# A top-32 search on VectorE: the order of two rows' instructions in a step is changed, with two candidate buffers, and two small operations are rewritten

## The chip, the cores and the metric

The kernel runs on one core of one Trainium2 chip. A core has five engines that run side by side: TensorE (PE, with its weight loads as PEld), VectorE (DVE), ScalarE (ACT), GpSimd (POOL) and SyncE (SP), which here issues most of the DMAs. Each engine works through its own list of instructions in order and waits on semaphores where it needs another's result, or an earlier one of its own. The metric is the device time of one execution in microseconds (us); smaller is better.

## The reference

An attention whose softmax keeps only the 32 largest scores of each row is followed by a mixture of eight experts with one expert per token. Cut to what matters:

```python
scores = (q @ k.transpose(0, 1, 3, 2)) / np.sqrt(64)        # 8 batches, 8 heads, 576 x 576
kth = np.partition(scores, -32, axis=-1)[..., -32:-31]
scores = np.where(scores >= kth, scores, -1e9)
attn = softmax(scores); x = attn @ v                        # rows of 512, 4608 tokens
logits = x @ w_gate; e = argmax(logits)                     # one of 8 experts
out = softmax(logits)[e] * (np.maximum(x @ w1[e], 0) @ w2[e])
```

The part that concerns us is finding, for each of the 8 x 8 x 576 score rows, the 32 largest of 576 values.

## The kernel before

**Tiling and stages.** The score rows are worked in 144 steps (`NQ * NT` = 16 x 9). A step t holds two tiles of 128 rows by 576 scores, called row 0 and row 1 here. The loop at L1004 issues, in each pass t, work of several steps at once: the scores of step t+3 on PE (L1012 to L1017), copied into an `sb` pair by ACT; the top-32 search of step t on DVE; the mask of step t-2 (a Sign on ACT at L454 and an add of 576 columns on POOL at L455); the transposes of step t-3 on PE (L461), the exponentials (L467) and the product with v (L477) after that. The experts follow the attention; there the work is mostly matmuls (L1153, L1168).

**The search of one step** (`topk`, L407). Row 0 is cut into 11 chunks and row 1 into 10 (`CHUNKS`). A MAX8 on each chunk (list `one`, run at L1025) writes its 8 largest values into a candidate tile, `cand0` (88 columns) or `cand1` (80 columns). The candidates are laid out so that column groups hold the chunks' first, second, ... largest values. Then each row has four rounds on its candidates (list `two`, run at L1033): a MAX8 gives 8 of the 32 values into `vq`, and a match_replace takes these 8 out of the candidates before the next round. On the chip a match_replace is two instructions, MATCH_VALUE_LOAD, which reads the 8 values just found, and MATCH_REPLACE8. The rounds read 22, 33, 77 and 88 columns of row 0 and 20, 40, 70 and 80 of row 1 (`RANKS`). So a row has seven entries in `two`, written in this text as a0 to a6 for row 0 (a0, a2, a4, a6 are MAX8, a1, a3, a5 match_replace) and b0 to b6 for row 1. Each entry needs the one before it of its own row. The order before is a0 b0 a1 b1 ... a6 b6, behind all 21 chunks. The chunks are called c0 to c20 (c0 to c10 of row 0).

**Small instructions.** Other jobs put small DVE instructions into a queue (`vec`, `dq`). From the third entry of `two` on, one of them is issued behind each entry (L1034), and what is left behind the last entry. In some steps the queue is empty, in others it holds up to 27.

**Behind the search.** `last`, a small POOL operation that makes two biases `nb` out of `vq`, is kept as `delayed` and issued at the start of the next pass (L1007). In the last step of a group of nine a TENSOR_REDUCE `mx_n` (L430) is added behind b6.

**Two small operations** matter as well. `settle` (L440) computes a shift for several groups: one scalar_tensor_tensor of 3 columns for each group, with `slope` and `level` as its two tensors. `j_find` (L656) computes a list of places `r_fl`, one column, as li[:,1] * 37 + li[:,0], with a scalar_tensor_tensor whose two tensors are two columns of `r_li`. It runs once in each of the eight batches.

Of the kernel before, what the change touches and what calls it, by code (L numbers as in the profile page):

```python
# [8 lines left out]
F32 = mybir.dt.float32  # L9
# [5 lines left out]
OP = mybir.AluOpType  # L15
# [5 lines left out]
NEG = -3.0e38  # L21
BELOW = 1.0 - 2.0 ** -24
TOPK = 32
# [25 lines left out]
def attention_moe(ctx, tc, q, k, v, w_gate, w1, w2, out):  # L49
    nc = tc.nc  # L50
# [37 lines left out]
    NT = 2 * MAIN + 1  # L88
# [6 lines left out]
    work = att.enter_context(tc.tile_pool(name="work", bufs=2))  # L95
# [53 lines left out]
    NLT = HP * (2 * MAIN + 1)  # L149
# [18 lines left out]
    for i in range(3):  # L168
        t = consts.tile([128, S], BF, name=f"sg{i}")
# [20 lines left out]
    shift = consts.tile([128, NQ, 3], F32, name="shift")  # L190
    slope = consts.tile([128, 3], F32, name="slope")
    nc.vector.memset(slope, 1.0)
    nc.vector.memset(slope[:, 0:1], -0.125)
    level = consts.tile([128, 3], F32, name="level")
# [18 lines left out]
    for p in range(HP):  # L213
        for h in range(2):
            hd = 2 * p + h
            w = 2 * MAIN + 1
            t0 = 1 + (p // 2) * 2 * w + (h if p % 2 == 0 else w + 1 + h)
            a = attr[:, t0:t0 + 2 * MAIN - 1:2, :]
# [4 lines left out]
            a = attr[h * LEFT:(h + 1) * LEFT, tl_, :]  # L223
# [8 lines left out]
    for i in range(3):  # L232
        t = work.tile([128, 2, KW], F32, name=f"qk{i}", bufs=1)
# [11 lines left out]
    for i in range(2):  # L245
        t = jobs.tile([128, NLT + 1, 2], F32, name=f"nb{i}", bufs=1)
# [32 lines left out]
    def flush(queue):  # L279
        while queue:  # L280
            queue.pop(0)()
# [60 lines left out]
    def grp(t):  # L342
        if t < 0 or t >= steps:
            return []
        n, s = divmod(t, NT)
        p = 2 * n
        if s < MAIN:
            return [p * NT + s, p * NT + MAIN + s]
        if s == MAIN:
            return [p * NT + 2 * MAIN, (p + 1) * NT + 2 * MAIN]  # L350
        s -= MAIN + 1
        return [(p + 1) * NT + s, (p + 1) * NT + MAIN + s]
# [54 lines left out]
    def topk(t, us):  # L407
        n, s = divmod(t, NT)
        if s == 0:
            VQ[n] = jobs.tile([128, 2 * NT, TOPK], F32, name="vq")  # L410
        v = VQ[n][:, 2 * s:2 * s + 2, :]
        one, two, cand = [], [], {}
        for i, u in enumerate(us):
            nc_ = CHUNKS[i]
            cand[i] = work.tile([128, 8 * nc_], F32, name=f"cand{i}", bufs=1)
            for c in range(nc_):
                one.append((nc.vector.max, (cand[i][:, c::nc_], SB[u][:, edges[i][c]:edges[i][c + 1]])))

        for r in range(TOPK // 8):
            w = [cand[i][:, 0:CHUNKS[i] * RANKS[i][r]] for i in range(2)]  # L420
            for i in range(2):
                two.append((nc.vector.max, (v[:, i, 8 * r:8 * r + 8], w[i])))
            if r < TOPK // 8 - 1:
                for i in range(2):
                    two.append((nc.vector.match_replace, (w[i], v[:, i, 8 * r:8 * r + 8], w[i], NEG)))
        b, lt = divmod(t, 2 * NT)
        nb = NB[t] = NBB[b % 2][:, 1 + 2 * lt:3 + 2 * lt]
        if s == NT - 1 and n + 4 < NQ:
            MX[n] = jobs.tile([128, 1], F32, name="mx_n")
            two.append((nc.vector.tensor_reduce, (MX[n], VQ[n][:, :, 0], AX.X, OP.max)))  # L430

        last = (nc.gpsimd.tensor_tensor, (nb, v[:, :, 0:TOPK:TOPK - 1], factors, OP.mult))
        return one, two, last
# [6 lines left out]
    def settle(pt, ns, done):  # L440
        mm = jobs.tile([128, 1], F32, name="mm")
        vec(nc.vector.tensor_reduce, mm, pt[:, 0:128], axis=AX.X, op=OP.max)
        vec(done)
        for n in ns:
            vec(nc.vector.scalar_tensor_tensor, shift[:, n], slope, mm, level, op0=OP.mult, op1=OP.add)

    SHIFTED = {0, 1, 2, 3}

# [165 lines left out]
    def j_find(b):  # L614
        sm = lambda name, shape, dt=F32: jobs.tile(shape, dt, name=name, bufs=1)
        yield need(dve=0.3)
        while (b + 1) * NLT // (2 * NT) - 1 not in CHECKED:
            yield
        key = sm("r_key", [128, NLT])
        vec(nc.vector.scalar_tensor_tensor, key, CNT[b], float(2 * TOPK - S), idx1, op0=OP.not_equal, op1=OP.mult)  # L620
        vec(nc.vector.max, rhs[:, :, 0], key)
        ok = sm("r_ok", [128, 9], BF)
        vec(nc.vector.tensor_scalar, ok[:, 0:8], rhs[:, :, 0], 0.0, None, op0=OP.is_gt, op1=OP.add,
            accum_out=ok[:, 8:9])
        nbb = NBB[b % 2]
        ntab = dram.tile([128 * (NLT + 1), 2], F32, name=f"ntab{b}")
        nc.sync.dma_start(ntab.rearrange("(p t) a -> p t a", p=128), nbb)
        yield need(spot=1, pe=0.1)
        pr, leave = spot("stat")
        pe(nc.tensor.matmul, pr[:, 0:1], before, ok[:, 8:9], start=True, stop=True)  # L630
        pe(nc.tensor.matmul, pr[:, 1:3], ones, ok[:, 7:9], start=True, stop=True)
        act(nc.scalar.activation, stat[:, b], pr[:, 0:3], AF.Copy)
        if 2 * b + 4 < NQ:
            spread(pr[:, 128:256])
            settle(pr[:, 128:256], [2 * b + 4, 2 * b + 5], leave)
            SHIFTED.update([2 * b + 4, 2 * b + 5])
        else:
            act(leave)
        yield need(slack=1)
        yield need(dve=1.3)  # L640
        sl = sm("r_sl", [128, 8], BF)
        vec(nc.vector.scalar_tensor_tensor, sl, slots[:, 0:8], stat[:, b, 0:1], ok[:, 0:8], op0=OP.add, op1=OP.mult)
        oh = sm("r_qx", [128, 512]).bitcast(BF).rearrange("p (j x) -> p j x", j=8)
        vec(nc.vector.tensor_tensor, oh, slots[:, None, :].to_broadcast([128, 8, 128]),
            sl[:, :, None].to_broadcast([128, 8, 128]), op=OP.is_equal)
        yield need(spot=1, pe=0.5)
        pl, leave = spot("li")
        for j in range(8):
            pe(nc.tensor.matmul, pl[:, 0:2], oh[:, j], rhs[:, j], start=(j == 0), stop=(j == 7))
        li = sm("r_li", [128, 2])  # L650
        act(nc.scalar.activation, li, pl[:, 0:2], AF.Copy)
        act(leave)
        yield need(slack=1)
        yield need(dve=0.1)
        fl = sm("r_fl", [128, 1], I32)
        vec(nc.vector.scalar_tensor_tensor, fl, li[:, 1:2], float(NLT + 1), li[:, 0:1], op0=OP.mult, op1=OP.add)  # L656
        yield need(pool=2.0)
        at = sm("r_at", [128, 4], I32)
        pool(nc.gpsimd.indirect_dma_start, out=at, out_offset=None, in_=atab,
             in_offset=bass.IndirectOffsetOnAxis(ap=fl[:, 0:1], axis=0))  # L660
        nb = jobs.tile([128, 8], F32, name="r_nb", bufs=3)
        pool(nc.gpsimd.indirect_dma_start, out=nb[:, 0:2], out_offset=None, in_=ntab,
             in_offset=bass.IndirectOffsetOnAxis(ap=fl[:, 0:1], axis=0))
        yield need(pool=1.8)
        qi = jobs.tile([128, 2], I32, name="r_qi", bufs=3)
        pool(nc.gpsimd.tensor_scalar, qi, at[:, 0:3:2], b * H * S, None, op0=OP.add)
        sb = jobs.tile([128, S], F32, name="r_sb", bufs=2)
        pool(nc.gpsimd.indirect_dma_start, out=sb, out_offset=None, in_=SCD[b],
             in_offset=bass.IndirectOffsetOnAxis(ap=at[:, 0:1], axis=0))
        hf = sm("r_hf", [128, 1])  # L670
        pool(nc.gpsimd.tensor_copy, hf, at[:, 1:2])
        hm = jobs.tile([128, H], F32, name="r_hm", bufs=3)
        pool(nc.gpsimd.tensor_scalar, hm, eight, hf, None, op0=OP.is_equal)
        hmb = hm[:, :, None].to_broadcast([128, H, D])
        pool(nc.gpsimd.tensor_scalar, used[:, b:b + 1], hf, float(H), None, op0=OP.is_lt)
        yield need(pool=0.7)

        low = nb[:, 2:3]
        pool(nc.gpsimd.tensor_scalar, nb[:, 3:4], nb[:, 1:2], 1.0 + 2.0 ** -10, None, op0=OP.mult)
        pool(nc.gpsimd.tensor_scalar, low, nb[:, 0:1], -(2.0 ** -7), None, op0=OP.mult)  # L680
        pool(nc.gpsimd.tensor_tensor, low, low, nb[:, 3:4], op=OP.add)
        FOUND[b] = (sb, nb, qi, hmb)
# [314 lines left out]
    if NQ > 1:  # L997
# [2 lines left out]
    prep(2)  # L1000
    AHEAD = [(A0, ahead_load, (0,)), (A0, ahead_load, (1,)), (A1, ahead_take, ()), (A2, ahead_split, (0,)),
             (A3, ahead_split, (1,))]
    delayed = None
    for t in range(steps + LAG + TD + 4):  # L1004
        n, s = divmod(t, NT)
        if delayed:
            delayed[0](*delayed[1])  # L1007
        if grp(t - LAG - TD - 1):
# [10 lines left out]
            transp(t - LAG - TD)  # L1019
        flush(pq)  # L1020
        flush(aq)
        one, two, last = topk(t, grp(t)) if grp(t) else ([], [], None)
        for m in range(max(len(one), 1)):
            if m < len(one):
                one[m][0](*one[m][1])  # L1025
        delayed = last
        if t == 1:
            settle(first_pt, [0, 1, 2, 3], lambda: release(first_pt))
            mine_, dq[:] = dq[:], []
            flush(mine_)  # L1030
        mine, dq[:] = dq[:], []
        for m, (f, a) in enumerate(two):
            f(*a)  # L1033
            if mine and m >= 2:  # L1034
                mine.pop(0)()
# [458 lines left out]
```

## Time and profile before

| what | value |
|---|---|
| median of the runs | 1287.82 us (three runs, 1287.07 to 1288.76) |
| the profiled execution's own time | 1287.93 us |
| its span, first to last instruction | 1286.1 us |
| DVE busy | 1032.4 us in the span |
| first and last chunk MAX8 of the search | 12.8 us and 752.2 us |
| MAX8 on chunks | 3024 (144 x 21) |

The attention takes the time up to some 755 us; the experts take the rest. The profile is of one execution; its time lies 0.11 us above the median of the runs. In a row of the timeline the first number is the start in us from the span's start, the second how long the merged group lasted; then come the engine, the line of the kernel, the operation, the tiles and shapes and how many instructions were merged (x2). Two DVE instructions overlap in such rows: the next one starts before the one ahead has ended, so the cost of one on its engine is the distance from its start to the next start, and not its length.

### The profile page before, as it was taken

To read this page: it belongs to the slowest core of one execution; us is meant where nothing else is said; L and a number is where in the kernel's file an instruction comes from. 1 tells how busy PE (TensorE), PEld (TensorE's weight loads), DVE (VectorE), ACT (ScalarE), POOL (GpSimd) and SP (SyncE) were. 2 spreads that over 40 slices of the span, in tenths; PEclk is the share of its full clock that TensorE was granted. 3 is DMA by queue.
4 is the path that set the end of the run, shared out by engine and by line. 5 is a ranking of instruction groups with operands and counts; after the bars stand their busy time and mean duration, and the time that the engine had idled before them with its cause. 6 is when DMAs were issued, how large, how long until landed. Compare 5 with 4: busy or idle time off the path is not lost.

```text
span 1286.1 us, 31773 instructions
## 1 busy us (share of the span) xinstructions
PE 1211.3 (94%) x9126; PEld 962.8 (75%) x9126; DVE 1032.4 (80%) x6907; ACT 831.2 (65%) x1699; POOL 840.5 (65%) x1213
## 2 busy tenths in 40 slices
PE   6999999999999999999999879899999999999997
PEld 3667667766666676666766668788999898899996
DVE  7999999999999999999999987756674333446555
ACT  4999798888888888888988853333333232334433
POOL 4676766767867867867967858765655142445654
PEclk8999999999999999999999999899999999999999
DMA  6765565655655655655654635646565243556773
GB/s 169 234 177 184 172 192 154 187 172 160 179 172 160 184 169 169 180 173 155 204 172 140 185 98 156 205 130 182 163 185 177 70 131 90 164 162 186 231 211 114
DMA packets 276759, 215.38 MB, mean 167 GB/s; under 512 B 136617, under 2 KB 218713, under 8 KB 276576
## 3 DMA queue, kind: packets, MB, share of 16 engines
q1 hardware_dynamic: 265840, 190.11, 50.1%
q0 software_dynamic: 9504, 22.86, 5.7%
q8 instruction: 74, 1.21, 0.4%
q14 instruction: 109, 0.89, 0.2%
q10 hardware_dynamic: 1232, 0.30, 0.1%
HBM read 106.69 MB, written 107.90 MB: 167 GB/s over the span
## 4 chain that ended last, share of the span: by engine, by line
DVE 51%; PE 37%; issue 3%; POOL 3%; DMA 2%; ACT 2%; SPq 1%; POOLq 0%; ACTq 0%; DVEq 0%
DVE cand L1025 25%; PE ph L1153 17%; PE y L1168 17%; DVE cand L1033 11%; DVE vq L1033 9%; PE mt L1133 1%; PE pt L265 1%; DVE xm L265 1%; POOL sb L455 1%; POOL wl L957 1%; ACT sg L454 1%; DVE r_v L265 1%; DMA rk<-in_k_dram 1%; DVE r_qx L265 1%; SPq L113 0%
## 5 line engine op out<-in xcount | busy, mean ns | idle before, releaser
L455 POOL TENSOR_TENSOR sb<-sb,sg 128x576 f32<-128x576 f32 x288 | 370.4, 1303 | 43.2 <-ACT sg L454 39.7
L1025 DVE MAX8 cand<-sb 128x8 f32<-128x52 f32 (+2 forms) x3024 | 368.3, 207 | 0.2 <-issue 0.2
L957 POOL TENSOR_TENSOR wl<-r,wh 128x512 fp32r<-128x512 f32 x118 | 152.7, 1295 | 206.3 <-DVE wh L956 202.0
L454 ACT ACTIVATE sg<-sb,nb 128x576 int8<-128x576 f32 x288 | 229.2, 796 | 61.0 <-POOL sb L455 60.5
L1154 ACT ACTIVATE hh<-ph 128x256 fp32r<-128x256 f32 (+3 forms) x136 | 58.2, 428 | 247.4 <-PE ph L1153 209.7
L477 PEld LDWEIGHTS px<-et,rv 128*64 128x64 f32 x2688 | 129.2, 137 | 118.4 <-ACT xt L265 50.4
L1033 DVE MAX8 vq<-cand 128x8 f32<-128x22 f32 (+7 forms) x1152 | 200.2, 204 | 0.0
L461 PE MATMUL tt<-turner,sb 128*128 128x128 f32 x1296 | 176.0, 277 | 22.6 <-POOL sb L455 17.9
L367 PE MATMUL ps<-qk 64*128 64x512 f32 (+1 forms) x576 | 183.7, 646 | 4.3 <-ACT sb L369 3.5
L1155 DVE SCALAR_TENSOR_TENSOR hl<-ph,hh 128x256 fp32r<-128x256 f32 (+3 forms) x136 | 65.0, 478 | 151.3 <-ACT hh L1154 131.9
L467 ACT ACTIVATE et<-tt,shift 128x1152 f32<-128x1152 f32 x144 | 178.3, 1238 | 1.5 <-PE tt L461 1.5
L477 PE MATMUL px<-et,rv 128*64 128x128 f32 (+1 forms) x2688 | 162.2, 266 | 11.2 <-ACT xt L265 8.7
L461 PEld LDWEIGHTS tt<-turner,sb 128*128 128x128 f32 x1296 | 145.6, 143 | 35.7 <-POOL sb L455 29.0
L1153 PE MATMUL ph<-xh,wh 128*128 128x256 f32 (+3 forms) x536 | 169.8, 317 | 0.0
L1153 PE MATMUL ph<-xh,wl 128*128 128x256 f32 (+3 forms) x536 | 165.8, 309 | 0.0
L1153 PE MATMUL ph<-xl,wh 128*128 128x256 f32 (+3 forms) x536 | 165.3, 308 | 0.0
L1033 DVE MATCH_REPLACE8 cand<-vq,cand 128x22 f32<-128x22 f32 (+2 forms) x864 | 158.5, 189 | 0.0
L369 ACT ACTIVATE sb<-ps 128x1024 f32<-128x1024 f32 x144 | 149.1, 1035 | 8.1 <-PE ps L367 8.1
L1168 PE MATMUL y<-wh,hl 128*128 128x512 f32 x324 | 128.4, 396 | 1.4 <-DVE skip L265 1.4
L1168 PE MATMUL y<-wl,hh 128*128 128x512 f32 x324 | 128.2, 396 | 0.0
L1168 PE MATMUL y<-wh,hh 128*128 128x512 f32 x324 | 128.2, 396 | 0.0
L1153 PEld LDWEIGHTS ph<-xh,wh 128*128 128x128 f32 x536 | 101.6, 190 | 4.2 <-issue 1.3
(260 smaller groups left out, 2183.4 us busy)
## 6 DMA issues: line engine op xcount, KB each, us to landing
r<-in_moe_w_dram SPq DMA_DIRECT2D x236, 256.0 KB
sc<-sb SPq DMA_DIRECT2D x128, 288.0 KB
sc<-sb SPq DMA_DIRECT2D x128, 256.0 KB
rv<-in_v_dram SPq DMA_DIRECT2D x32, 256.0 KB
xs<-xm SPq DMA_DIRECT2D x16, 512.0 KB
rq<-in_q_dram SPq DMA_DIRECT2D x60, 128.0 KB
rk<-in_k_dram SPq DMA_DIRECT2D x60, 128.0 KB
sc<-sb SPq DMA_DIRECT2D x32, 144.0 KB
```

Source lines behind the costliest of these rows:

```text
L367: nc.tensor.matmul(MAINS[:, n], qk[:, 0, w], qk[:, 1, 2 * LEFT:], start=True, stop=True)
L369: nc.scalar.activation(bass.AP(EX[-1].tensor, EX[-1].offset, [list(EX[-1].ap[0]), [S + LEFT, 2], [1, M]]), MAINS, AF.Copy)
L454: nc.scalar.activation(upper(SG[i]), SB[u], AF.Sign, bias=nb[:, i, 1:2], accum_out=CNT[b][:, 2 * lt + i:2 * lt + i + 1])
L455: nc.gpsimd.tensor_tensor(SB[u], SB[u], SG[i], op=OP.add)
L461: nc.tensor.matmul(tt[:, c], x[:, c * 128:(c + 1) * 128], ident, start=True, stop=True, is_transpose=True)
L467: nc.scalar.activation(ET[t], three.rearrange("p (c q) -> p c q", c=NB9), AF.Exp, bias=shift[:, t // NT, 0:1], scale=0.125)
L477: yield lambda kb=kb, blk=blk: nc.tensor.matmul(px[h * 64:(h + 1) * 64], block(rv, p % 2, kb if kb < MAIN else MAIN + n, h), et[:, blk, q] ...
L957: ((other or nc.gpsimd) if i else nc.vector).tensor_tensor(lo, r, hi, op=OP.subtract)
L1025: one[m][0](*one[m][1])
L1033: f(*a)
L1153: nc.tensor.matmul(ph, a[:, c, :], x[:, c, s], start=(m == 0), stop=(m == len(seq) - 1))
L1168: nc.tensor.matmul(PY[u, t], a[:, s], x, start=(f == 0 and m == 0), stop=(f == FC - 1 and m == 2))
```

## The change

Four things are done.

1. The order. c0 of a step is issued first in the pass, ahead of `delayed` and the rest. Behind it comes b6 of the step before (`carry`). Then c1 to c18 follow, and `two` is now a0 c19 a1 c20 a2 b0 a3 b1 a4 b2 b3 a5 b4 a6 b5. In the last step of a group of nine, b6 is not carried but follows b5 directly, and `mx_n` follows where there is one.
2. `cand0` and `cand1` have two buffers each, used in turn by the steps.
3. `settle` writes the shifts of all its groups with one instruction, with `slope` and `level` broadcast over the groups.
4. `r_fl` is computed by a tensor_scalar, with one column of `r_li` as its tensor and the other as its scalar operand for each partition.

The diff in full, but for context lines:

```diff
-        one, two, cand = [], [], {}
+        one, two, cand, rounds = [], [], {}, ([], [])
...
-            cand[i] = work.tile([128, 8 * nc_], F32, name=f"cand{i}", bufs=1)
+            cand[i] = work.tile([128, 8 * nc_], F32, name=f"cand{i}", bufs=2)
...
             for i in range(2):
-                two.append((nc.vector.max, (v[:, i, 8 * r:8 * r + 8], w[i])))
-            if r < TOPK // 8 - 1:
-                for i in range(2):
-                    two.append((nc.vector.match_replace, (w[i], v[:, i, 8 * r:8 * r + 8], w[i], NEG)))
+                rounds[i].append((nc.vector.max, (v[:, i, 8 * r:8 * r + 8], w[i])))
+                if r < TOPK // 8 - 1:
+                    rounds[i].append((nc.vector.match_replace, (w[i], v[:, i, 8 * r:8 * r + 8], w[i], NEG)))
+        a, b = rounds
+        two += [a[0], one.pop(-2), a[1], one.pop()]
+        for i in range(len(a) - 4):
+            two += [a[i + 2], b[i]]
+        two += [b[-4], a[-2], b[-3], a[-1], b[-2], b[-1]]
...
-        for n in ns:
-            vec(nc.vector.scalar_tensor_tensor, shift[:, n], slope, mm, level, op0=OP.mult, op1=OP.add)
+        k = len(ns)
+        vec(nc.vector.scalar_tensor_tensor, shift[:, ns[0]:ns[0] + k], slope[:, None, :].to_broadcast([128, k, 3]), mm,
+            level[:, None, :].to_broadcast([128, k, 3]), op0=OP.mult, op1=OP.add)
...
-        vec(nc.vector.scalar_tensor_tensor, fl, li[:, 1:2], float(NLT + 1), li[:, 0:1], op0=OP.mult, op1=OP.add)
+        vec(nc.vector.tensor_scalar, fl, li[:, 1:2], float(NLT + 1), li[:, 0:1], op0=OP.mult, op1=OP.add)
...
-    delayed = None
+    delayed, carry = None, []
     for t in range(steps + LAG + TD + 4):
         n, s = divmod(t, NT)
+        one, two, last = topk(t, grp(t)) if grp(t) else ([], [], None)
+        if one:
+            f, a = one.pop(0)
+            f(*a)
+        flush(carry)
         if delayed:
...
-        one, two, last = topk(t, grp(t)) if grp(t) else ([], [], None)
         for m in range(max(len(one), 1)):
...
         mine, dq[:] = dq[:], []
+        if two and s < NT - 1:
+            f, a = two.pop()
+            carry.append(lambda f=f, a=a: f(*a))
         for m, (f, a) in enumerate(two):
```

## The prediction

> **What bounds the kernel now.** I read the page first: busy time by engine, the slices over time, and the chain that ended last.
>
> ```profile
> PE 1211.3 (94%) x9126; PEld 962.8 (75%) x9126; DVE 1032.4 (80%) x6907; ACT 831.2 (65%) x1699; POOL 840.5 (65%) x1213
> ...
> DVE  7999999999999999999999987756674333446555
> ...
> DVE 51%; PE 37%; issue 3%; POOL 3%; DMA 2%; ACT 2%; SPq 1%; POOLq 0%; ACTq 0%; DVEq 0%
> DVE cand L1025 25%; PE ph L1153 17%; PE y L1168 17%; DVE cand L1033 11%; DVE vq L1033 9%; PE mt L1133 1%; PE pt L265 1%; DVE xm L265 1%; POOL sb L455 1%; POOL wl L957 1%; ACT sg L454 1%; DVE r_v L265 1%; DMA rk<-in_k_dram 1%; DVE r_qx L265 1%; SPq L113 0%
> ```
>
> PE is the busiest over the span, but that is an average of two stages. In the attention DVE stands at 9 in every slice, and 45% of the last chain is the search (L1025 and L1033). Next come the waits of DVE between 30 and 740 us, and one stretch of the windows (columns: length, then PE, PEld, DVE busy).
>
> ```profile
> DVE mm L265 <- ACT stat L265: 1.5, 1, 1.5
> DVE cand L1025 <- issue: 0.2, 1, 0.2
> ```
> ```profile
> 399.00:494.00 95.00, 89.12 (x796) 64.92 (x795) 95.00 (x803) 82.27 (x172) 73.21 (x110) 1.00 0.59 172
> ```
>
> DVE waited 1.7 us in 710 for anybody else. So each nanosecond added to or taken from a step on DVE counts, 144 times. PE has 5.9 us of 95 free: a DVE gain of more than 6% would meet it, and this change can't bring that much. The order within DVE decides.
>
> **How much a dependence costs.** These are single DVE rows of a step with no small instructions (step 85, 445.71 to 450.29, 4.58 us).
>
> ```profile
> 445.53 0.23 DVE L1033 MAX8 vq<-cand 128x8 f32<-128x80 f32 x1
> 445.71 0.22 DVE L1025 MAX8 cand<-sb 128x8 f32<-128x52 f32 x1
> 448.06 0.21 DVE L1025 MAX8 cand<-sb 128x8 f32<-128x58 f32 x1
> 448.18 0.17 DVE L1033 MAX8 vq<-cand 128x8 f32<-128x22 f32 x1
> 448.31 0.18 DVE L1033 MAX8 vq<-cand 128x8 f32<-128x20 f32 x1
> 448.62 0.17 DVE L1033 MATCH_REPLACE8 cand<-vq,cand 128x20 f32<-128x20 f32 x1
> 448.70 0.18 DVE L1033 MAX8 vq<-cand 128x8 f32<-128x33 f32 x1
> 448.81 0.20 DVE L1033 MAX8 vq<-cand 128x8 f32<-128x40 f32 x1
> 450.29 0.23 DVE L1025 MAX8 cand<-sb 128x8 f32<-128x52 f32 x1
> ```
>
> Chunks, which need nothing of each other, follow at 0.12 us (20 distances from 445.71 to 448.06). The 20-wide replace at 448.62 is followed after 0.08. But b0 at 448.31 comes 0.13 behind a0, which is 22 wide: it needs c20, which ended at 448.27, and starts 0.04 later. It is also longer than the wider a0, by about 0.02. So b0 is held: 0.05 + 0.02, less rounding, 0.06 us. b2 at 448.81 is held in the same way by b1, which ended at 448.79: 0.11 behind a 33-wide a2 instead of some 0.095, and 0.02 longer, 0.035 us. The clean measure of a direct dependence is a chain of eight adds of one column.
>
> ```profile
> 925.19 1.51 DVE L1249 TENSOR_TENSOR cum<-cum,ov 128x1 f32<-128x1 f32 x8
> ```
> ```profile
> L1249 DVE TENSOR_TENSOR cum<-cum,ov 128x1 f32<-128x1 f32 x8 | 1.3, 159 | 0.3
> ```
>
> (1.51 - 0.16) / 7 = 0.193 from start to start, for a length of 0.159: the next starts 0.034 after the end of the one it needs. A held instruction is 0.018 longer, so it counts as end + 0.034 to 0.052. The price of a step's order is then worked out from lengths and distances.
>
> **A rule against it.** The Trainium skill ("VectorE: DVE Perf Modes", The DRAIN you can't avoid) says that the next operation waits for the pipeline to empty anyway, and that a semaphore between chained operations adds nothing. By that rule neither spacing nor a lost wait would matter. The trace disagrees, 0.12 between free chunks of length 0.21 against 0.193 in the dependent chain; the rule stays as a rival below.
>
> **Removed by the order.** b0's hold: 144 x 0.06 = 8.6 us. b2's hold: where no small instruction lies between, in 56 steps (the first and the last by their c0), 56 x 0.035 = 2.0.
>
> ```profile
> 22.76 0.22 DVE L1025 MAX8 cand<-sb 128x8 f32<-128x52 f32 x1
> ...
> 738.47 2.56 DVE L1025 MAX8 cand<-sb 128x8 f32<-128x52 f32 x21
> ```
>
> **Removed by the second buffer.** c0 overwrites candidates that a6 of the step before has just read, and also needs ACT's copy of the scores. As I read it, the second wait makes the extra instruction ahead of it.
>
> ```profile
> L1025 DVEq EVENT_SEMAPHORE  x108: 21/21/21, 17.3 to 749.8; - x108
> ```
> ```profile
> 410.12 0.23 DVE L1033 MAX8 vq<-cand 128x8 f32<-128x80 f32 x1
> 410.26 0.20 DVE L1025 MAX8 cand<-sb 128x8 f32<-128x52 f32 x1
> ```
>
> Where it is missing (410.26), c0 follows b6 after 0.14 and is 0.20 long; where it stands (445.71), 0.18 and 0.22. So it costs 0.06, x 108 = 6.5 us. With two buffers the reader is two steps back, and DVE has waited past it since: I take all 6.5; if the wait stays, none.
>
> **Added by the order.** I go through the new row of instructions with the same prices.
> - b3 stands directly behind b2, whose result its MATCH_VALUE_LOAD reads. b2 unheld is 0.18 long, so the load starts 0.18 + 0.034 to 0.052 after it instead of 0.10: held 0.118 to 0.136 us. No row shows this pair; the nearest is the chain above, and I take 0.13. At the low end it could be nothing, if the load doesn't wait as adds do. Eight small instructions are needed before one falls between b2 and b3; that is so in 14 steps (from the one at 181 us, with redo's list, to the last). 130 x 0.13 = 16.9 us (0, or 15.3 to 17.7).
> - b0 now has c20 and a2 ahead, 0.12 + 0.095 = 0.215; c20's end is at 0.21 + 0.034 to 0.052: held 0.03 to 0.05, in the 56 steps, 1.7 to 2.8; with small instructions none.
> - a3 behind a2 and b0: a2's 0.18 + 0.034 to 0.052 against 0.095 + 0.03 + 0.08, 0.01 to 0.03, in up to 97 steps: 1.0 to 2.8. a1 behind a0 and c19: 0.17 + 0.034 to 0.052 against 0.20, up to 0.015: 0 to 2.2.
> - b6 behind b5 and the next c0: the 70-wide replace is 0.217 long, and 0.133 + 0.114 lie between: held 0 to 0.02, 128 times, 0.5 to 2.8. In the 16 last steps of a group it stands directly behind b5: 16 x 0.13 = 2.1.
> - The small instructions, often dependent on each other, have shorter neighbours than before: 0 to 2, I take 1. c19 and c20 only change place.
>
> ```profile
> L1033 DVE MATCH_REPLACE8 cand<-vq,cand 128x70 f32<-128x70 f32 x144 | 31.2, 217 | 0.0
> ```
>
> In the middle 16.9 + 2.3 + 1.9 + 1.1 + 1.7 + 2.1 + 1.0 = 27.0, against 17.1 removed. **The order alone costs 9.9 us**; with each end 5 to 16.
>
> **Places from one tensor.**
>
> ```profile
> 325.23 2.52 POOL L455 TENSOR_TENSOR sb<-sb,sg 128x576 f32<-128x576 f32 x2
> ```
> ```profile
> 326.34 1.43 DVE L265 SCALAR_TENSOR_TENSOR r_fl<-r_li 128x1 int32<-128x1 f32 x1
> 327.70 0.08 DVE L1033 MATCH_VALUE_LOAD cand<-vq,cand 128x8 f32 x1
> ```
> ```profile
> L265 DVE SCALAR_TENSOR_TENSOR r_fl<-r_li 128x1 int32<-128x1 f32 x8 | 8.9, 1108 | 0.0
> L265 DVE SCALAR_TENSOR_TENSOR r_fl<-r_li x8: 150/1420/1433, 141.8 to 791.8; 128x1 int32<-128x1 f32 x8
> L265 DVE TENSOR_SCALAR r_nb<-r_nb x8: 137/140/146, 208.7 to 831.5; 128x1 f32<-128x1 f32 x8
> ```
>
> One column takes 1.43 us and ends when POOL's adds do (325.23 + 2.52 = 327.75); unhindered it takes 0.15. A tensor_scalar of one column, r_nb, is never over 0.146. Saved: 8.9 - 8 x 0.15 = 7.7, of which the eighth lies among the experts, so 7/8, 6.7 us. The Trainium skill ("SBUF — State Buffer", Who interferes with whom) has the same lock for two SBUF inputs, but counts tensor_scalar in a two-port mode among those that contend; by that r_fl would keep its 6.7. The r_nb row speaks against it.
>
> **Shifts in one.**
>
> ```profile
> 20.12 0.62 DVE L265 SCALAR_TENSOR_TENSOR shift<-slope,mm,level 128x3 f32<-128x3 f32 x4
> ...
> 301.28 0.35 DVE L265 SCALAR_TENSOR_TENSOR shift<-slope,mm,level 128x3 f32<-128x3 f32 x1
> 301.56 0.19 DVE L1033 MAX8 vq<-cand 128x8 f32<-128x40 f32 x1
> 301.67 0.20 DVE L265 SCALAR_TENSOR_TENSOR shift<-slope,mm,level 128x3 f32<-128x3 f32 x1
> 301.79 0.08 DVE L1033 MATCH_VALUE_LOAD cand<-vq,cand 128x8 f32 x1
> ```
>
> The second of a pair costs 301.79 - 301.67 = 0.12, in six batches 0.7; the first time three of four go, 3 x 0.13 = 0.4. The first one's own hold stays. 1.1 us.
>
> **What hangs on b6.** POOL's nb waits for b6, which now ends about 0.25 us later in the step; behind nb stand POOL's two adds, and for those wait ACT's Sign and PE's transposes.
>
> ```profile
> POOL nb L1007 <- DVE vq L1033: 69.7, 39, 3.8
> ```
> ```profile
> 743.31 2.52 POOL sb L455 x2
> ```
>
> POOL waited for it 39 times with 1.8 us on average, and DVE never waits for POOL's result, so I cost this at nothing until the last 30 us, where the chain runs through POOL (743.31). There the last step's b6 isn't carried. What the delay can cost is that POOL's adds lie 0.25 later over the remaining small two-input instructions: about a dozen, 0 to 3 us, and I take 1. No DMA is issued in another order; SP's queue is as before.
>
> **Sum.** 9.9 + 1 - 6.7 - 1.1 = +3.1 us; DVE's time goes through to the end as the chain shows. 1287.93 + 3.1 = 1291.0 for the profiled execution; the median stands 0.11 lower, so 1290.9. By the ends, 5 - 7.8 = -3 to 16 + 3 - 7.8 = +11.
>
> **The rivals.**
> - The load isn't held behind b2. Then 16.9 go: 1274 us; the kernel turns faster once the load is held under 0.106 us, 3.1 / 130 less than the 0.13 taken. Against it: every dependent pair in the trace has the 0.034 behind the end.
> - The rule of no price for semaphores, as a mechanism: holds and the extra instruction are only other names for time spent anyway. Then the order does nothing and 7.8 are gained: 1280. Against it: 0.14 and 0.18 ahead of c0.
> - The second buffer doesn't take the extra wait away, because the new c0 or b6 still has two to wait for: 6.5 more, 1297. It decides if more than about half of the 108 remain.
> - The holds cancel: those at a1, a3, b6 and in the small instructions are at their low ends: 1288. For it: most of them sit within 0.02 of nothing.
>
> **How the numbers follow.** About 0.2% (2.6 us) is what a measurement of this kernel can tell from no change. Forecast, with +1 to +11: 0.55. Load not held: 0.09. No price at all: 0.08. Wait stays: 0.10. Cancelled, 1285 to 1289: 0.18. The range from 1280 to 1298 leaves out the first rival and the upper tail. Slower by over 0.2%: 0.40 of the forecast and 0.09 of the stayed wait, 0.49. Faster: 0.09 + 0.08 and 0.03 of the cancelled, 0.20. Within: the rest, 0.31.
>
> **What would show it.** In the profile after: no EVENT_SEMAPHORE at the chunk line; r_fl near 0.15; the load of b3 0.21 to 0.24 behind its 40-wide MAX8; a step with no small instructions of 4.60 to 4.66 us against 4.58 with the extra instruction and 4.52 without. The forecast is wrong if that load follows within 0.12, or if DVE begins to wait for others in the attention.

## The result, and the profile after

| | before | after |
|---|---|---|
| median of the runs | 1287.44 us (4 runs) | 1303.12 us (4 runs, 1302.13 to 1304.01) |
| profiled execution, its span | 1287.93, 1286.1 us | 1303.89, 1302.1 us |
| 143 steps of the search, from the first chunk of one to that of the next | 737.1 us | 753.3 us |

The ratio is 1.0122, with an interval of 1.0104 to 1.0139. The forecast was 1290.9 us with a range of 1280 to 1298: the direction was right, the size was not.

The last row is worked out from the trace. Each DVE instruction is charged the distance from its start to the next DVE start, and these distances are summed from c0 of the first step to c0 of the last. This sum rose by 16.2 us, which is the whole rise of the span (16.0): the experts behind the search gave nothing and took nothing. From the page after, busy time, slices over time, and the two rows of the chain that ended last:

```profile
PE 1222.3 (94%) x9126; PEld 968.4 (74%) x9126; DVE 1044.2 (80%) x6898; ACT 835.3 (64%) x1699; POOL 841.9 (65%) x1213
...
DVE  7999999999999999999999996755674333446555
...
DVE 53%; PE 36%; POOL 3%; issue 3%; DMA 2%; ACT 1%; SPq 1%; POOLq 0%; ACTq 0%; DVEq 0%
DVE cand L1034 21%; PE ph L1165 17%; PE y L1180 16%; DVE cand L1045 14%; DVE vq L1045 8%; POOL sb L460 1%; PE mt L1145 1%; DVE vq L1043 1%; DVE cand L1014 1%; DVE xm L265 1%; PE pt L265 1%; DVE r_qx L265 1%; POOL wl L962 1%; DMA sc<-sb 1%; DVE r_v L265 0%
```

DVE is still what ends last in the attention, and it now has 9s for one slice more. It is as full as before and does nine instructions fewer, so the time lies within its own row of instructions: holds. Summed by kind in the same way (us):

| | before | after | difference | forecast |
|---|---|---|---|---|
| chunks and rounds | 652.8 | 664.6 | +11.8 | +8.9 |
| r_fl | 7.3 | 0.85 | -6.5 | -6.7 |
| shift | 3.3 | 4.2 | +0.9 | -1.1 |
| r_qx | 7.9 | 13.05 | +5.1 | in the next row |
| all other small instructions | 65.7 | 70.6 | +4.9 | +2.0, with r_qx |

The **order** of chunks and rounds did nearly what was expected of it. Here is the clean step from 255.88 us in the timeline of after:

```profile
255.88 0.21 DVE L1014 MAX8 cand<-sb 128x8 f32<-128x52 f32 x1
256.01 0.24 DVE L1043 MAX8 vq<-cand 128x8 f32<-128x80 f32 x1
...
259.44 0.18 DVE L1045 MAX8 vq<-cand 128x8 f32<-128x40 f32 x1
259.66 0.09 DVE L1045 MATCH_VALUE_LOAD cand<-vq,cand 128x8 f32 x1
259.74 0.18 DVE L1045 MATCH_REPLACE8 cand<-vq,cand 128x40 f32<-128x40 f32 x1
...
260.40 0.21 DVE L1045 MATCH_REPLACE8 cand<-vq,cand 128x70 f32<-128x70 f32 x1
260.54 0.21 DVE L1014 MAX8 cand<-sb 128x8 f32<-128x52 f32 x1
```

The step is 4.66 us long, the upper end of the forecast's 4.60 to 4.66. The load of b3 starts 0.22 behind its 40-wide MAX8, which ends at 259.62. In the views of the lines that issue chunks (L1014 for c0, L1034 for c1 to c18) the rows stand alone after, with no EVENT_SEMAPHORE below them; nor is there one at L1045, which issues c19 and c20:

```profile
L1014 DVE MAX8 cand<-sb x144: 202/212/221, 12.8 to 766.1; 128x8 f32<-128x52 f32 x144
L1034 DVE MAX8 cand<-sb x2592: 198/206/223, 12.9 to 768.3; 128x8 f32<-128x52 f32 x67, 128x8 f32<-128x58 f32 x45, 128x8 f32<-128x53 f32 x44, 128x8 f32<-128x57 f32 x44
```

The **small instructions** are where it went otherwise. The tile views give the shortest, the median and the longest instruction in ns; first before, then after:

```profile
L265 DVE TENSOR_TENSOR r_qx<-slots,r_sl x8: 1207/1210/1225, 127.0 to 781.4; 128x1024 bf16<-128x1024 bf16 x8
L265 DVE SCALAR_TENSOR_TENSOR r_key<-cnt,idx x8: 183/185/304, 110.1 to 774.9; 128x36 f32<-128x36 f32 x8
L265 DVE SCALAR_TENSOR_TENSOR shift<-slope,mm,level x16: 196/215/753, 20.1 to 587.3; 128x3 f32<-128x3 f32 x16
```
```profile
L265 DVE TENSOR_TENSOR r_qx<-slots,r_sl x8: 1204/2233/2244, 128.8 to 797.9; 128x1024 bf16<-128x1024 bf16 x8
L265 DVE SCALAR_TENSOR_TENSOR r_key<-cnt,idx x8: 184/436/669, 111.2 to 791.4; 128x36 f32<-128x36 f32 x8
L265 DVE SCALAR_TENSOR_TENSOR shift<-slope,mm,level x7: 231/753/784, 20.0 to 599.5; 128x6 f32<-128x6 f32 x6, 128x12 f32<-128x12 f32 x1
```

Instructions of the same shape have become longer: r_qx by 1.02 us, r_key by 0.25. All of them read two tensors in SBUF, as r_fl did, which the prediction had seen held until POOL's adds end. What POOL was doing shows in the timelines of step 93 (c0 at 488.82 us before, 499.14 after). Before:

```profile
488.99 0.20 POOL L1007 TENSOR_TENSOR nb<-vq,factors 128x4 f32<-128x4 f32 x1 [1.89 <-DVE vq L1033]
489.14 2.51 POOL L455 TENSOR_TENSOR sb<-sb,sg 128x576 f32<-128x576 f32 x2
491.62 0.79 POOL L265 TENSOR_TENSOR vq<-vq 128x288 f32<-128x288 f32 x1
492.08 0.35 DVE L265 SCALAR_TENSOR_TENSOR shift<-slope,mm,level 128x3 f32<-128x3 f32 x1
```

After:

```profile
499.59 0.20 POOL L1017 TENSOR_TENSOR nb<-vq,factors 128x4 f32<-128x4 f32 x1 [2.18 <-DVE vq L1043]
499.74 2.53 POOL L460 TENSOR_TENSOR sb<-sb,sg 128x576 f32<-128x576 f32 x2
502.21 0.81 POOL L265 TENSOR_TENSOR vq<-vq 128x288 f32<-128x288 f32 x1
502.30 0.75 DVE L265 SCALAR_TENSOR_TENSOR shift<-slope,mm,level 128x6 f32<-128x6 f32 x1
```

nb, which waits for b6, starts 0.17 us into the step before and 0.45 after; the adds end 2.83 and 3.13 into it. The first shift moves the other way, from 3.26 to 3.16, and in both traces it ends where POOL's next two-input instruction ends (492.43 and 492.41; 503.05 and 503.02). So one hold of 0.35 us has become one of 0.75, and that is more than the change saved by dropping the second shift.

**The theory**, A: a wait of DVE on its own result is paid at the earlier instruction's end plus 0.034 to 0.052 us. And a small instruction with two SBUF tensors is held while POOL runs one of its own, so its price hangs on when POOL's chain nb, add, add (some 2.7 us from b6's end) is over, against the time at which the small instruction stands in the step. **The rivals**: the small instructions cost by their place among the rounds, whatever POOL does; the order costs more in the rounds than the clean step shows; the carried b6 is what costs.

### The profile page after: what moved, and what is told of

It is laid out like the page before. It is cut to its first block, busy times and chain, and to the rows that moved or that the text cites. A ratio compares the mean times of both kernels' runs of the same rounds, so it can differ in the third digit from the quotient of the medians.

```text
span 1302.1 us, 31657 instructions
## 1 busy us (share of the span) xinstructions
PE 1222.3 (94%) x9126; PEld 968.4 (74%) x9126; DVE 1044.2 (80%) x6898; ACT 835.3 (64%) x1699; POOL 841.9 (65%) x1213
## 3 DMA queue, kind: packets, MB, share of 16 engines
q8 instruction: 74, 1.21, 0.4%
## 4 chain that ended last, share of the span: by engine, by line
DVE 53%; PE 36%; POOL 3%; issue 3%; DMA 2%; ACT 1%; SPq 1%; POOLq 0%; ACTq 0%; DVEq 0%
DVE cand L1034 21%; PE ph L1165 17%; PE y L1180 16%; DVE cand L1045 14%; DVE vq L1045 8%; POOL sb L460 1%; PE mt L1145 1%; DVE vq L1043 1%; DVE cand L1014 1%; DVE xm L265 1%; PE pt L265 1%; DVE r_qx L265 1%; POOL wl L962 1%; DMA sc<-sb 1%; DVE r_v L265 0%
## 5 line engine op out<-in xcount | busy, mean ns | idle before, releaser
L1034 DVE MAX8 cand<-sb 128x8 f32<-128x52 f32 (+3 forms) x2592 | 315.3, 207 | 0.0
L466 PE MATMUL tt<-turner,sb 128*128 128x128 f32 x1296 | 181.1, 279 | 31.7 <-POOL sb L460 22.3
L1045 DVE MAX8 vq<-cand 128x8 f32<-128x22 f32 (+7 forms) x1024 | 175.8, 200 | 0.5
L1045 DVE MATCH_REPLACE8 cand<-vq,cand 128x22 f32<-128x22 f32 (+2 forms) x864 | 160.1, 189 | 0.0
```

The costliest lines, as they stand in the source:

```text
L466: nc.tensor.matmul(tt[:, c], x[:, c * 128:(c + 1) * 128], ident, start=True, stop=True, is_transpose=True)
```

## The experiments

The medians of the kernel before, taken again beside the runs below, were 1288.00 (the first four runs), 1287.94 (the next four) and 1287.86 us (the last two). "Small" and "rounds" are the sums over 143 steps made as above; "rounds" leaves out the chunks, which stay within 351 to 353 us: 299.7 before, 311.6 after. Small is 84.3 before and 88.7 after.

### 1. The second buffers alone

```diff
-            cand[i] = work.tile([128, 8 * nc_], F32, name=f"cand{i}", bufs=1)
+            cand[i] = work.tile([128, 8 * nc_], F32, name=f"cand{i}", bufs=2)
```

> The kernel before with two candidate buffers and nothing else. Theory A (what a semaphore wait costs on DVE is paid): the second wait ahead of c0, 108 extra instructions of 0.06 us, goes and nothing takes its place: 1281 us (1280 to 1282.5), no EVENT_SEMAPHORE at the chunk line. Rival (the extra instruction is hidden behind the end of the last MAX8): 1287, the clean step stays at 4.58 us.

Measured 1283.96 us, 0.9975 (0.9965 to 0.9984). The chunk line's rows in its view:

```profile
L1025 DVE MAX8 cand<-sb x3024: 191/206/222, 12.8 to 748.0; 128x8 f32<-128x52 f32 x63, 128x8 f32<-128x58 f32 x54, 128x8 f32<-128x57 f32 x36, 128x8 f32<-128x53 f32 x36
```

The EVENT_SEMAPHOREs are gone, and chunks and rounds fell from 652.8 to 646.3: the 6.5 us of the forecast to the digit. But the small instructions rose by 2.3 (r_fl by 1.1, r_key by 0.7), which gave a third of it back, and the time lies above the expected range. Without the EVENT_SEMAPHORE behind b6, everything on DVE comes 0.06 us sooner after b6, and so earlier against POOL's chain, which starts at b6. That fits theory A.

### 2. The other three edits without the order

Second buffers, shift and r_fl as in the change, the order as before.

> The changed kernel with the old order of the search: two buffers, one shift instruction, places from one tensor. Theory A: 6.5 us from the wait, 6.5 from r_fl, about 1 from the shifts: 1273.5 us (1272 to 1276). So the order alone would be worth some 29 us of loss in the changed kernel. Rival: the hold that r_fl had on POOL's adds passes to the next small instruction, and only the wait is gained: 1280.

Measured 1277.29 us, 0.9929 (0.9909 to 0.9948); rounds 295.0, small 79.3. That lies between theory A's range and the rival's 1280. r_fl gained all it should, so its hold did not pass on as the rival had it; but other small instructions rose by some 2.6 us, as they did in run 1. So these edits are worth 10.7 us, and the order takes 25.8 (1303.12 - 1277.29). In the sums over the steps the order alone is 18.7 us in chunks and rounds (645.9 to 664.6) and 9.4 in the small instructions (79.3 to 88.7). The prediction had the order at 9.9 with the 6.5 of the second buffers in it, so 16.4 without.

### 3. nb behind the two adds in POOL's list

```diff
-        if delayed:
-            delayed[0](*delayed[1])
...
+        if delayed:
+            delayed[0](*delayed[1])
         if grp(t - LAG - TD - 2):
```

> The changed kernel, but POOL's nb is issued behind the two adds of the same pass, so that the adds no longer wait for the carried b6. Theory A (the small two-input instructions lose time because POOL's adds lie 0.3 us later in the step): the small instructions of 143 steps take about 79 us of DVE instead of 88.7, rounds as in the changed kernel: 1293 us (1290 to 1297). Rival B (they lose it because of their new places among the rounds and chunks): 1303, small instructions still 88 us.

Measured 1311.18 us, 1.0183 (1.0162 to 1.0204): slower where it should have been faster. Of the small instructions, those that theory A named went free: r_key sums to 0.81 us (2.75 after), shift to 1.34 (4.22). But others came under the adds, which no longer stand at one place in the step; r_sl rose from 1.35 to 6.38 and r_v from 8.05 to 12.99, and small as a whole from 88.7 to 93.8. Step 95 (c0 at 511.26) in this kernel's timeline:

```profile
514.00 1.32 DVE L265 SCALAR_TENSOR_TENSOR r_sl<-slots,stat,r_ok 128x8 bf16<-128x8 bf16 x1
515.37 2.25 DVE L265 TENSOR_TENSOR r_qx<-slots,r_sl 128x1024 bf16<-128x1024 bf16 x1
514.02 2.51 POOL L460 TENSOR_TENSOR sb<-sb,sg 128x576 f32<-128x576 f32 x2
516.49 1.18 POOL L1024 TENSOR_TENSOR nb<-vq,factors 128x4 f32<-128x4 f32 x1
```

r_sl handles eight columns and takes 1.32 us. In this step POOL has a list of its own first, and without nb ahead of them the adds now start right beside r_sl. The number was a miss, since I had thought only of the steps in which POOL has nothing else. That a small instruction waits where POOL's adds stand fits these rows, but the gain that theory A forecast did not come.

### 4. b6 never carried

```diff
-        if two and s < NT - 1:
+        if False:
```

> The changed kernel without the carry: b6 stands directly behind b5 in every step. Theory A: 128 more direct holds of 0.13 instead of 0.02, +14 us on DVE, but POOL's nb and adds lie 0.3 us earlier again, and r_key, po, hist and shift are as fast as before, -6 us: 1311 us (1308 to 1314). Rival B: the small instructions stay slow: 1317.

Measured 1316.46 us, 1.0235 (1.0214 to 1.0256): outside theory A's range, and at the rival's number. The end of a clean step in its timeline:

```profile
257.35 0.22 DVE L1045 MATCH_REPLACE8 cand<-vq,cand 128x70 f32<-128x70 f32 x1
257.60 0.25 DVE L1045 MAX8 vq<-cand 128x8 f32<-128x80 f32 x1
257.76 0.20 DVE L1014 MAX8 cand<-sb 128x8 f32<-128x52 f32 x1
```

b6 starts 0.25 behind the replace instead of 0.13, and is 0.25 long against 0.226 when nothing holds it. Rounds rose by 14.1 to 325.7, which prices a direct pair once more at 14.1 / 127 = 0.11 us. The carry therefore doesn't cost: it saves 13 us in this order. Nor do the small instructions come back to 84 (87.9), although nb starts 0.17 into the step again. With b6 no longer ahead of the chunks the first of them starts earlier too, 2.57 us into the step (median) against 2.84 before. So undoing b6's delay did not give the small instructions back. What theory A had left out is that they move as well, and that only the distance between them and the adds counts: in steps in which POOL's nb starts early, with no other list ahead of it, the first small instruction starts 0.04 us behind the end of the adds in the kernel before, 0.38 ahead of it after and 0.27 ahead of it in this run (medians).

### 5. Two entries carried, and nothing directly behind b2

```diff
-        two += [b[-4], a[-2], b[-3], a[-1], b[-2], b[-1]]
+        two += [a[-2], b[-4], a[-1], b[-3], b[-2], b[-1]]
```

Here `carry` takes b5 and b6, issued c0 b5 c1 b6.

> The changed kernel with b2 and b3 apart: ... a4 b2 a5 b3 a6 b4, and b5 and b6 are both carried, behind c0 and c1 of the next step. Theory A: the hold of b3 behind b2 (16 us) shrinks to small holds, rounds of 143 steps about 300 us of DVE instead of 311.6; POOL's nb waits 0.27 us longer, and the small two-input instructions lose about 5 us more: 1297 us (1293 to 1302). Rival (the direct pair isn't where the time went): 1303 or more, rounds unchanged.

Measured 1291.83 us, 1.0027 (1.0017 to 1.0038). From its timeline, the load of a5, which now stands behind b2 in place of b3's, and then r_qx of step 95 with POOL beside it:

```profile
255.58 0.33 DVE L1050 MAX8 vq<-cand 128x8 f32<-128x77 f32 x2
255.85 0.09 DVE L1050 MATCH_VALUE_LOAD cand<-vq,cand 128x8 f32 x1
...
504.09 1.21 DVE L265 TENSOR_TENSOR r_qx<-slots,r_sl 128x1024 bf16<-128x1024 bf16 x1
504.11 2.33 POOL L460 TENSOR_TENSOR sb<-sb,sg 128x576 f32<-128x576 f32 x1
```

The distances behind the 40-wide MAX8 fell from 29.6 to 16.4 us in sum, 13.2 less, or 0.092 apiece: the pair of b2 and b3 is gone, and a5's load still waits 0.02 for a4. Some of it was given back at other places, so that the rounds fell by 7.8. r_qx is back at 1.21: it starts just ahead of the add, and this time it is the add that lasts 2.33 us in place of some 1.28. Small fell by 6.0 (r_qx by 5.2, shift by 2.8, while others rose), where theory A had wanted some 5 more for the later nb: a miss, and the reason why the time lies below its range. Later adds are thus not always worse; r_qx got ahead of them. By the medians 11.3 us came back.

### 6. The small instructions later, in the changed kernel

```diff
-            if mine and m >= 2:
+            if mine and m >= 6:
```

> The changed kernel, but the small instructions begin behind a3 (seventh entry) instead of behind a1. Theory A, in the form that the runs so far give it (POOL's nb and two adds take some 2.7 us from the end of b6; a two-input instruction that comes sooner on DVE is held until they end): r_key, po, shift and hist are free again, about 6 us less; r_qx is held 0.5 us less each, 3 us; b0 and a3 are no longer covered by small instructions, 5 us more: 1299 us (1295 to 1303). Rival (the places among the rounds matter, not the time since b6): the small instructions still take 88 us or more: 1307.

Measured 1289.81 us, 1.0013 (1.0003 to 1.0023): a number in the loop's condition takes back 13.3 of the 15.7 us, more than theory A's range had it. Steps 93 and 95 in its timeline:

```profile
494.65 0.21 DVE L265 SCALAR_TENSOR_TENSOR shift<-slope,mm,level 128x6 f32<-128x6 f32 x1
...
504.41 0.22 DVE L265 SCALAR_TENSOR_TENSOR r_sl<-slots,stat,r_ok 128x8 bf16<-128x8 bf16 x1
504.70 1.22 DVE L265 TENSOR_TENSOR r_qx<-slots,r_sl 128x1024 bf16<-128x1024 bf16 x1
504.69 1.28 POOL L1017 TENSOR_TENSOR nb<-vq,factors 128x4 f32<-128x4 f32 x1
```

shift takes 0.21 instead of 0.75, r_qx 1.22, and it is nb, on POOL, that is held. Small fell by 10.0 to 78.7. The rounds, expected to cost 5 more, fell by 4.1: a small instruction stands between b2 and b3 more often now (the sum behind the 40-wide MAX8 went from 29.6 to 27.2).

### 7. The small instructions earlier, in the kernel before

```diff
-            if mine and m >= 2:
+            if mine and m >= 0:
```

> The kernel before, but the small instructions begin behind a0 instead of a1, about 0.25 us sooner, with the order, the buffers and the forms untouched. Theory A: r_key, po, shift and hist are held by POOL's adds as in the changed kernel, small instructions about 5 us more than 84.3; b0's hold is covered where there is one, 4 to 5 us less: 1288 us (1284 to 1292). Rival (small instructions lose time only from the new order): small instructions unchanged, 1283.

Measured 1291.26 us, 1.0022 (1.0012 to 1.0031). Small rose by 4.8 as theory A wanted (shift 3.3 to 5.0, hist's tensor_tensor 2.4 to 3.5, po 1.1 to 2.0), with no other change. That the rounds would fall by 4 to 5 us, as small instructions cover b0's hold, was a miss: they fell by 0.4. Behind a0 and b0 the distances lost 0.7 in sum, but behind b1's replace and behind b2 they gained 1.2.

### 8 and 9. Fillers from the next step

To take the holds out, two chunks of the next step (c0', c1') go between the rounds, on the kernel of the second run: a0 c0' b0 a1 b1 a2 c1' b2 a3 b3 and so on.

```diff
+        one, two, last = ahead_
+        ahead_ = topk(t + 1, grp(t + 1)) if grp(t + 1) else ([], [], None)
+        if two and ahead_[0]:
+            two.insert(1, ahead_[0].pop(0))
+            two.insert(6, ahead_[0].pop(0))
...
-            if mine and m >= 2:
+            if mine and m >= 3:
```

> The version without the new order (two buffers, r_fl, shifts), with two chunks of the next step moved forward as fillers: a0 c0' b0 a1 b1 a2 c1' b2 and on as before; small instructions from a1 on. Theory A: the holds of b0 (0.06) and b2 (0.035) go, and no pair stands directly: rounds and chunks of 143 steps 10 us less than without the fillers; POOL's adds lie some 0.15 later against the small instructions, 1 to 3 us: 1269 us (1265 to 1274). Rival (the holds overlap with something that ends anyway): 1277.

Measured 1274.35 us, 0.9893 (0.9876 to 0.9909). That is just above the range. A clean step has no hold left and takes 4.42 us, and chunks and rounds fell by 9.4 us against run 2, of the 10 expected. Small was 83.1, of which shift 3.1 and hist 3.1: the meeting with POOL again, which the next run tests in the same order (`m >= 7` in place of `m >= 3`).

> The kernel of the run with two fillers, its small instructions from the eighth entry of the two rows on (behind b2, some 0.5 us later in the step) instead of the fourth. If what is left of the loss there is the meeting with POOL's adds (r_v, shift and hist, about 1.8, 2.4 and 2.4 us above their free sums), most of it goes and the list r_wk at the end of the step costs up to 2.4 more: small instructions 83 to 79 us, time 1270 (1268 to 1273). If the place of a small instruction doesn't matter, 1274 as there.

Measured 1268.41 us, 0.9856 (0.9841 to 0.9871), the fastest of all, and faster than both kernels. Small fell to 76.1. From its timeline:

```profile
249.87 0.17 DVE L1039 MAX8 vq<-cand 128x8 f32<-128x22 f32 x1
249.96 0.20 DVE L1039 MAX8 cand<-sb 128x8 f32<-128x52 f32 x1
250.07 0.16 DVE L1039 MAX8 vq<-cand 128x8 f32<-128x20 f32 x1
```

b0 now follows its neighbour with 0.11 between, and is 0.16 long instead of 0.18: the hold of before is gone.

### 10. r_fl alone

```diff
-        vec(nc.vector.scalar_tensor_tensor, fl, li[:, 1:2], float(NLT + 1), li[:, 0:1], op0=OP.mult, op1=OP.add)
+        vec(nc.vector.tensor_scalar, fl, li[:, 1:2], float(NLT + 1), li[:, 0:1], op0=OP.mult, op1=OP.add)
```

> The kernel before with r_fl alone rewritten as a tensor_scalar. If one column with a scalar operand isn't held by POOL's adds and nothing else moves, r_fl goes from 7.3 to 0.85 us in the search: 1281.5 (1280.5 to 1282.5). The rival: the instruction behind r_fl in the queue meets the adds in its place and takes over a part of the wait: 1284 to 1287.

Measured 1282.90 us, 0.9967 (0.9957 to 0.9977), between the two cases. The tile views of r_fl and r_wk in this kernel:

```profile
L265 DVE TENSOR_SCALAR r_fl<-r_li x8: 195/203/206, 143.6 to 790.5; 128x1 int32<-128x1 f32 x8
L265 DVE TENSOR_TENSOR r_wk<-sg,r_sb x8: 746/864/1773, 182.3 to 810.3; 128x576 f32<-128x576 bf16 x8
```

r_fl itself gained the whole 6.5 us, although it still stands under POOL's adds. But r_wk, which reads two SBUF tensors eight steps later, cost 1.2 more in two of its seven batches (its median was 749), each of them starting under one of POOL's adds, and ebase, held once, 1.0. Chunks and rounds were 2.0 longer in this trace, whose execution took 1285.03 us, 2.1 more than the median. r_wk isn't the instruction behind r_fl in the queue, which the rival had named; why those two batches were hit stays open.

## Why the prediction was right and wrong

- **Bound.** Right. After the change DVE waited in the search for others once, for 1.4 us, and every hold on it reached the end.
- **Price of a dependence.** Right, to the hundredth. Means over clean steps of the two traces, against the same instructions in run 9, where nothing is held (distance to the next start, and the excess length of the held one, which delays the next): b0 0.061 us (0.06 forecast), b2 0.034 (0.035), the EVENT_SEMAPHORE 0.062 (0.06), b3's load 0.136 (0.13), b0 in its new place 0.042 (0.03 to 0.05), b6 behind the next c0 0.022 (0 to 0.02). Carried to all steps that gave +11.8 for chunks and rounds instead of +8.9, within the ends of 5 and 16 that were set for the order (the ends of its terms as listed add up to 3.5 and 15.3). The rest is small: the loads of a1 and a3 are held 0.016 each, and two or three chunks and rounds 0.009.
- **No price for semaphores**, the rule of the Trainium skill ("VectorE: DVE Perf Modes", The DRAIN you can't avoid) by which a semaphore between chained operations adds nothing, doesn't describe these traces. The section itself adds that a next operation which isn't held starts earlier, and the free chunks agree, at 0.114 us from start to start for a length of 0.204. Removing the 108 EVENT_SEMAPHOREs by a second buffer took 6.5 us from chunks and rounds, and a direct pair cost 0.09 to 0.14 us wherever one was made or undone (after, runs 4 and 5).
- **r_fl.** Right: 0.12 us apiece in the step, 6.5 saved, and a one-column tensor_scalar isn't held by POOL's adds. In run 10 its median was 0.203 us, where the tensors and the adds around it are those that had made the two-tensor form last 1.42. The form alone isn't what frees it, for wider ones are held. In the trace of before, r_v has a tensor_scalar with one tensor of eight columns and a column as its scalar:

```profile
463.86 0.34 DVE L265 TENSOR_SCALAR r_v<-eight,r_nb 128x8 f32<-128x8 f32 x1
462.54 1.64 POOL L455 TENSOR_TENSOR sb<-sb,sg 128x576 f32<-128x576 f32 x1 [0.39 <-ACT sg L454]
L265 DVE TENSOR_SCALAR r_v<-eight,r_nb x8: 209/338/744, 182.0 to 813.7; 128x8 f32<-128x8 f32 x8
```

It takes 0.21 when free; in 4 of the 7 batches within the search it took 0.34 and ended 0.02 to 0.03 us behind one of POOL's adds, as here (464.20 and 464.18). The Trainium skill ("SBUF — State Buffer", Who interferes with whom) counts tensor_scalar among those that contend only in a two-port mode, and there only when its operands meet that mode's conditions. So the prediction was too quick to say that by this page r_fl would keep its wait: r_v's eight columns fit the page, and r_fl's one column doesn't speak against it. In which mode either ran, no run here shows.
- **The failing step** is the price of the delayed b6: "POOL's adds lie 0.25 later over the remaining small two-input instructions: about a dozen, 0 to 3 us, and I take 1". The meeting with the adds and the delay were right (b6's nb starts 0.28 later in step 93), but the term was mis-sized. It measured some 11 us (r_qx 5.1, shift 0.9 and the others 4.9 in the table), of which the comparison with run 2 puts 9.4 on the order. Three things were left out. There are more such instructions than a dozen: 7 r_key, 5 po, 4 hist and 5 shift each grew by 0.25 to 0.40, 21 in all, 6 us. The first of them also stands 0.10 earlier in the step (2.74 us into it against 2.84), so that they move towards each other; to the other places of c19, c20 and b0 the prediction gave no such price. And r_qx, 1.13 us and never held in the trace of before, stood just at the edge: it lost its place in 5 of the 7 batches within the search, 1.03 us each, 5 us.
- **Shifts in one.** Wrong in sign, +0.9 for -1.1, by the same step: "The first one's own hold stays" should have said that it depends on where POOL stands. Where it stands free of POOL, one shift costs 0.12 and all seven together 1.25 (run 6), against 3.3 before: the edit itself is good.

The edge in which r_qx stood was there to be read in the trace of before. Step 95 in its timeline:

```profile
502.23 0.20 POOL L1007 TENSOR_TENSOR nb<-vq,factors 128x4 f32<-128x4 f32 x1
502.37 1.21 DVE L265 TENSOR_TENSOR r_qx<-slots,r_sl 128x1024 bf16<-128x1024 bf16 x1
502.38 3.57 POOL L455 TENSOR_TENSOR sb<-sb,sg 128x576 f32<-128x576 f32 x2
```

r_qx starts 0.01 us ahead of an add and takes its own 1.21, and the two adds take 3.57 where they take 2.5 in a step without it. The same step after:

```profile
513.21 3.49 POOL L460 TENSOR_TENSOR sb<-sb,sg 128x576 f32<-128x576 f32 x2
513.33 2.24 DVE L265 TENSOR_TENSOR r_qx<-slots,r_sl 128x1024 bf16<-128x1024 bf16 x1
```

Now the add is first by 0.12, and DVE pays. For POOL's two adds the outcome makes little difference (3.57 and 3.49); on DVE it is 1.03 us.

What is shown and what is argued: that the small instructions meet POOL, and that this makes some two thirds of the loss, is shown by runs 6 and 7 (the same instructions, only placed elsewhere: -10.0 and +4.8 us in their sum, of a loss of 15.7). The rival that the place among the rounds costs, whatever POOL does, has the traces against it. Of the 4790 small instructions of the search in all twelve traces, 333 lasted over 0.08 us longer than the shortest of their kind and shape; each of the 333 had an instruction of POOL beside it that ended first. What the theory could not do is forecast who is hit: the times lay outside its ranges in eight of the ten runs (1 to 6, 8 and 10; in the last two by 0.4 us). That b6's place alone moves POOL's adds is seen in the starts of nb, but it wasn't tried by itself; in run 4 the small instructions moved too, and how the loss divides between the two movements stays open.

## What to carry to other kernels

Before an instruction is moved on a full engine, list whom it releases on the others and what these then run beside the engine's own small instructions: here 0.3 us in POOL's adds and 0.1 in the small instructions cost some 11 us, while chunks and rounds, for which the order had been priced, cost 11.8. In the trace of before, look not only for the instructions that already pay for such a meeting but also for those that are just clear of it, by 0.01 us here, and put them where the other engine is done: moving the small instructions alone made 1303 into 1290 us (run 6) and 1274 into 1268 (run 9). Cover a dependent pair with work of another step that needs nothing, as in runs 8 and 9.

## What the runs showed of the hardware

- The meeting is an exclusion in both directions, one instruction at a time. In step 95 after, r_qx started under the first add, was done 1.08 us after that add's end, and the second add then lasted 2.25 us instead of 1.28. Whoever is second waits for the whole of the first one, even with eight columns of its own (r_sl 1.32 us).
- A tensor_scalar with a single tensor is held as well when it has eight columns (r_v, 0.21 us free and up to 1.20 in run 3) or two (skip, 0.15 free and 0.60 in the trace of before). With one column (r_fl, r_nb) it never took over 0.21 in the search in the twelve traces, though in 65 cases a tensor_tensor of POOL was running when they began and for at least 0.15 us more.
- Who wins isn't told by the starts in the trace when these are close: r_qx won with a start 9 ns ahead of the add before and 10 ns behind nb in run 6, while r_sl lost with a start 22 ns ahead of the add in run 3. In each case POOL's instruction before had not quite ended. What decides within some 20 ns stays open.
